# Ordering the second weight tile's conversion behind the first block's mean subtraction instead of behind the scaling of its input

## The chip, the cores and the metric

The kernel runs on one core of one Trainium2 chip. The metric is the device time of one execution in microseconds (us). Five engines matter: PE (TensorE, matrix products), DVE (VectorE), ACT (ScalarE), POOL (GpSimd) and SP, which here only issues transfers. Each engine works through its own instruction list in order.

## The reference

Three stages follow each other for 4 batches of 576 tokens.

```python
# 1. causal attention with a decay, 8 heads of 64
decay = cum[:, :, :, None] - cum[:, :, None, :]      # cum = cumsum(log f)
scores = np.where(causal, -1e9, q @ k.T / 8 + decay)
attn = softmax(scores);  x = concat_heads(attn @ v)  # 512 wide
# 2. normalised MLP, 512 -> 2048 -> 512
xn = (x - mu) / np.sqrt(var + 1e-6) * g_ln
x = x + np.maximum(xn @ w_ch1, 0.0) @ w_ch2
# 3. gated MLP with a product over the sequence
h = np.maximum(x @ w_in, 0.0);  u, v = split(h)
out = (u * (w_spatial @ layernorm(v) + b)) @ w_out
```

The weights arrive as float64 (two 32-bit words each) and are turned into float32 on the chip.

## The kernel before

**Blocks and groups.** The attention output is made in blocks of 256 tokens (`BLOCKS`), eight in all, and a ninth of the left-over tokens. The MLP of stage 2 runs on groups of blocks (`GROUPS`). Group 0 is block 0 alone and computes in float32; the later groups use pairs of float16 halves. Block 0 and block 1 hold the first 128 queries of two batches each (`attention32`, four head pairs); the next blocks use `attention1` and `attention`.

**Weight tiles.** The two weights of stage 2 are cut into 16 tiles (j = 0 to 15). Each tile is 1 MB of float64: `load_raw` loads it in two transfers into one of three buffers (`raw`), and `load_w` calls `narrow`, which has five steps:

- ACT takes the absolute value of the high words into `wt` (line 530, "Abs")
- ACT converts the low words into `low` (line 531)
- DVE clips `wt` (line 532)
- DVE puts the sign into `low` (line 533)
- DVE combines both into the float32 weight in `wt` (line 534)

In group 0 the hidden layer's products for tile j (line 707, into `ph`) and the second layer's (line 692, into `acc`) read the float32 weight. ACT's Relu (line 714) stands between them, and the second layer runs two tiles behind the first (`AHEAD`). After each conversion `squares(j)` multiplies the tile with itself (line 568, into `gram`); after tile 15 one small product of line 587 (`sums`) gives the scale of the weights, and `make16` (ACT line 597, DVE line 600) turns the tiles into float16 halves for group 1. On DVE, line 718 makes the low half of group 1's hidden layer.

**The norm of a block.** `norm` averages with a product (line 610), subtracts the mean with four DVE instructions (line 624), squares (ACT line 627), adds the squares on POOL (lines 631 and 632) and averages again (line 610). For group 0 `split` multiplies the centred block with the norm's gain g into `xg` (ACT line 671, four instructions); the products of line 707 read `xg`. The attention of a block ends with a copy of its last head pair into `xT` (ACT line 381).

**What sets the order.** `run` writes the steps down in the order of a list of due times (`SPAN`, `CONV`, `BEGIN`), and a scheduler with its own model of durations then sets the final order on each engine. `after(later, earlier)` adds an edge to it that keeps two instructions of one engine in order and makes no wait of its own. `PACE[j]` names the instruction behind which tile j's Abs must come: a place in `self.done`, or a name in `self.marks`. The mark "split" is the last scaling into `xg`.

Of the kernel before, what the change touches and what calls it, by code (L numbers as in the profile page):

```python
# [13 lines left out]
AF = mybir.ActivationFunctionType  # L14
ALU = mybir.AluOpType
# [38 lines left out]
SPAN.append((SPAN[-1][1] - 0.034, SPAN[-1][1] + 0.02))  # L54
RAWAT = (-0.975, -0.974, -0.973)
CONV = (-0.6, 0.001, 0.002, 0.003, 0.004)
PACE = (1, "split", "split", "split", "split")
LOWAT = (1, 2, 3)
SUMS = 13
SOON = 5  # L60
# [5 lines left out]
F64_LO = 2.0 ** -15  # L66
# [3 lines left out]
F64_HI = 2.0 ** 17 * (1 - 2.0 ** -5 - 2.0 ** -24)  # L70
# [10 lines left out]
def words(raw, w, dt):  # L81

    return raw.bitcast(dt).rearrange("p (n w) -> p n w", w=2)[:, :, w]


class Kernel:
# [236 lines left out]
    def attention32(self, b, xT):  # L323
        nc, at, bufs = self.nc, self.at, BUFS0
        mm = nc.tensor.matmul

        def bank(tag):
            return self.bank(tag).rearrange("p (b u w) -> p b u w", b=2, u=2)

        def four(tag):  # L330
            return at.tile([P, 2, 2, P], F32, tag=tag, name=tag, bufs=bufs[tag])
# [17 lines left out]
        for p in range(NP):  # L349
            qk, vr = qka[:, p], vra[:, :, p * P : (p + 1) * P]  # L350
            ps, e, diag = bank(tags[0]), four("e"), four("diag")
            st = at.tile([P, 2, 4], F32, tag="st", name="st", bufs=bufs["st"])
            four_ = [(n, u, 2 * n + u) for n in range(2) for u in range(2)]
            for n, u, c in four_:
                mm(ps[:, n, u], lhsT=qk[:, u, n, :P], rhs=qk[:, u, n, P:], start=True, stop=True, skip_group_check=True)
            for n, u, c in four_:
                mn, sm = st[:, 0, c : c + 1], st[:, 1, c : c + 1]
                nc.vector.tensor_tensor_reduce(
                    out=e[:, n, u], in0=ps[:, n, u], in1=self.mask[:, 512:], scale=-0.125, scalar=3e38, op0=ALU.add, op1=ALU.min, accum_out=mn)
                ex = nc.scalar.activation(e[:, n, u], e[:, n, u], AF.Exp, bias=mn, scale=-1.0, accum_out=sm)  # L360
                if b:
                    self.after(ex, self.marks["split"])
            nc.scalar.activation(st[:, 1], st[:, 1], AF.Copy, bias=1e-9)
            nc.vector.reciprocal(st[:, 1], st[:, 1])
            yield

            ps, pt = bank(tags[1]), four("PT")
            nc.vector.tensor_tensor(
                out=diag.rearrange("p n u w -> p (n u) w"), in0=self.ident.unsqueeze(1).broadcast_to([P, 4, P]),
                in1=st[:, 1].unsqueeze(2).broadcast_to([P, 4, P]), op=ALU.mult)  # L370
            for n, u, c in four_:
                mm(ps[:, n, u], lhsT=e[:, n, u], rhs=diag[:, n, u], start=True, stop=True, skip_group_check=True)
            copied = nc.scalar.activation(pt, ps, AF.Copy)
            if not b:
                self.done.append(copied)
            pav = bank("s2" if p % 2 and not b else tags[2])
            for n in range(2):

                for u in (1, 0):
                    mm(pav[: 64 * u + 64, 0, n], lhsT=vr[:, n, : 64 * u + 64], rhs=pt[:, n, u], start=True, stop=True, skip_group_check=True)  # L380
            nc.scalar.activation(xT[:, p].rearrange("p (n w) -> p n w", n=2), pav[:, 0], AF.Copy)
            if p == 1:
                xs = self.mo_sum(xT)
            elif p == 2:
                nc.vector.tensor_tensor(out=xs, in0=xs, in1=xT[:, 2, :], op=ALU.add)
            yield
# [130 lines left out]
    def narrow(self, raw, tmp, low=None):  # L517

        nc = self.nc
        a, b = tmp, tmp.bitcast(U32)  # L520
        lo, hi = words(raw, 0, U32), words(raw, 1, U32)
        if low is None:
            first = nc.scalar.activation(a, words(raw, 1, F32), AF.Abs)
            nc.vector.tensor_scalar(out=a, in0=a, scalar1=F64_LO, scalar2=F64_HI, op0=ALU.max, op1=ALU.min)
            nc.vector.tensor_scalar(out=b, in0=b, scalar1=3, scalar2=0x3FFFFFFF, op0=ALU.logical_shift_left, op1=ALU.bitwise_and)
            nc.vector.scalar_tensor_tensor(out=b, in0=hi, scalar=0xC0000000, in1=b, op0=ALU.bitwise_and, op1=ALU.bitwise_or)
            nc.vector.scalar_tensor_tensor(out=b, in0=lo, scalar=29, in1=b, op0=ALU.logical_shift_right, op1=ALU.bitwise_or)
        else:

            first = nc.scalar.activation(a, words(raw, 1, F32), AF.Abs, scale=2.0**16)  # L530
            self.low = nc.scalar.activation(low.bitcast(I32), lo, AF.Copy, scale=LOW)
            nc.vector.tensor_scalar(out=a, in0=a, scalar1=F64_LO * 2.0**16, scalar2=F64_HI * 2.0**16, op0=ALU.max, op1=ALU.min)
            nc.vector.scalar_tensor_tensor(out=low, in0=hi, scalar=0x80000000, in1=low, op0=ALU.bitwise_and, op1=ALU.bitwise_or)
            nc.vector.scalar_tensor_tensor(out=b, in0=b, scalar=3, in1=low, op0=ALU.logical_shift_left, op1=ALU.bitwise_or)
        return first
# [11 lines left out]
    def load_w(self, j):  # L547

        nc = self.nc
        if j not in self.raw:  # L550
            self.load_raw(j)
        raw, w = self.raw.pop(j), self.wt[:, j + 2]
        first = self.narrow(raw, w, self.st.tile([P, 2 * DM], U32, tag="low", name="low", bufs=2))
        at = PACE[j] if j < len(PACE) else NP + j - len(PACE)
        if at is not None:
            self.after(first, self.marks[at] if isinstance(at, str) else self.done[at])
        if j < len(LOWAT):
            self.after(self.low, self.done[LOWAT[j]])

# [53 lines left out]
    def norm(self, x, s, y, whole, end, c):  # L613


        nc, ns = self.nc, self.ns
        tag = "s" if end else "av"
        if s is None:
            pm = self.mean(tag, *(x[:, t] for t in range(NK)))
        else:  # L620
            nc.vector.tensor_tensor(out=s, in0=s, in1=x[:, 3, :], op=ALU.add)
            pm = self.mean(tag, s)
        for t in range(NK):
            nc.vector.tensor_tensor(out=c[:, t, :], in0=x[:, t, :], in1=pm, op=ALU.subtract)
        yield
        sq = ns.tile([P, NK, TOK], F32, tag="sq", name="sq", bufs=2)
        nc.scalar.activation(sq, c, AF.Square)
# [616 lines left out]
```

## Time and profile before

| What | Value |
|---|---|
| Median of 3 runs | 793.95 us (788.86 to 796.59) |
| The profiled execution | 790.01 us, of which the span is 788.3 us |
| PE busy | 761.2 us (97% of the span) |
| PE weight loads | 579.6 us (74%) |
| DVE busy | 555.3 us (70%) |
| ACT busy | 515.6 us (65%) |
| POOL busy | 59.7 us (8%) |

Shares are means over the whole span; the stages have different limits. The ends of PE's products are modelled, so a product's duration is longer than the spacing to the next. A float32 product leaves two records on PE, so "x8" of such products stands for four instructions of the program.

### The profile page before, as it was taken

How to read it: one execution, taken by the hardware profiler on the slowest of the kernel's cores; microseconds unless marked ns; L12 is line 12 of the kernel's file. 1: busy time of each engine (PE TensorE's matmuls, PEld its weight loads, DVE VectorE, ACT ScalarE, POOL GpSimd, SP SyncE). 2: the span in 40 equal slices, each digit the busy share in tenths (PEclk: the TensorE clock that was granted, in tenths of full speed). 3: DMA queues.
4: the chain of work that ended last, by engine and by line, in shares of the span. 5: the costliest groups of instructions: out<-in, count | busy, mean ns of one | idle time of the engine just before them, and what ended most of it. 6: DMA issues, size and time to landing. Idle time of an engine off the chain costs nothing.

```text
span 788.3 us, 16305 instructions
## 1 busy us (share of the span) xinstructions
PE 761.2 (97%) x5978; PEld 579.6 (74%) x5978; DVE 555.3 (70%) x1502; ACT 515.6 (65%) x1303; POOL 59.7 (8%) x89
## 2 busy tenths in 40 slices
PE   8799998999999999999999999999999999999997
PEld 6588887887877877778788888544447768667686
DVE  6699589849398989979958856687515672755725
ACT  5787389749388889888859844475425754556442
POOL 3100011011011001110201100100020000000000
PEclk8999999999999999999999999999999999999999
DMA  8888586367679997997995955730043230100101
GB/s 254 230 301 304 172 229 92 57 161 109 169 184 168 201 223 158 201 208 145 195 183 119 132 82 181 195 128 27 1 87 65 63 102 1 38 24 16 46 1 61
DMA packets 164227, 104.72 MB, mean 133 GB/s; under 512 B 106178, under 2 KB 151362, under 8 KB 164148
## 3 DMA queue, kind: packets, MB, share of 16 engines
q1 hardware_dynamic: 157848, 96.63, 50.8%
q0 software_dynamic: 5296, 5.28, 5.3%
q10 hardware_dynamic: 1004, 1.78, 0.8%
q8 instruction: 47, 0.77, 0.4%
q14 instruction: 32, 0.26, 0.1%
HBM read 64.37 MB, written 15.11 MB: 101 GB/s over the span
## 4 chain that ended last, share of the span: by engine, by line
PE 65%; DVE 12%; ACT 9%; DMA 8%; issue 3%; SPq 1%; POOL 1%; DVEq 0%; ACTq 0%; POOLq 0%
PE ph L707 15%; PE acc L692 13%; PE pb L647 8%; PE pb L648 8%; PE pb L649 8%; PE av L459 3%; PE s L295 2%; DMA PT<-P 2%; DVE P L316 2%; DMA vr<-in_v_dram 2%; PE s L692 1%; DVE sd L299 1%; ACT wt L597 1%; PE av L380 1%; DMA raw<-in_moe_w_in_dram 1%
## 5 line engine op out<-in xcount | busy, mean ns | idle before, releaser
L692 PE MATMUL acc<-hh,wt 128*128 128x256 f16 (+2 forms) x960 | 197.0, 295 | 0.8 <-DVE t L735 0.5
L707 PE MATMUL ph<-xh,wt 128*128 128x256 f16 (+1 forms) x896 | 186.7, 288 | 5.2 <-DVE hl L718 5.0
L707 PEld LDWEIGHTS <-wt 128*128 128x128 f16 x1344 | 126.8, 98 | 51.3 <-issue 13.2
L692 PEld LDWEIGHTS <-wt 128*128 128x128 f16 x1344 | 128.7, 98 | 43.9 <-issue 5.4
L707 PE MATMUL ph<-xl,wt 128*128 128x256 f16 (+1 forms) x448 | 129.0, 288 | 0.0
L692 PE MATMUL acc<-hl,wt 128*128 128x256 f16 (+1 forms) x416 | 115.2, 281 | 0.4 <-DVE hl L718 0.4
L714 ACT ACTIVATE hh<-ph 128x256 f16<-128x256 f32 (+2 forms) x128 | 51.0, 399 | 58.7 <-PE ph L707 58.5
L718 DVE SCALAR_TENSOR_TENSOR hl<-ph,hh 128x256 f16<-128x256 f32 (+1 forms) x112 | 50.6, 453 | 39.8 <-ACT hh L714 39.4
L260 ACT ACTIVATE P<-sd,st 128x512 f16<-128x512 f32 (+1 forms) x128 | 70.5, 586 | 10.5 <-DVE st L306 9.2
L316 DVE SCALAR_TENSOR_TENSOR P<-sd,st,P 128x384 f16<-128x384 f32 (+1 forms) x96 | 58.6, 633 | 9.3 <-ACT P L260 8.8
L303 ACT ACTIVATE sd<-sd,st 128x384 f32<-128x384 f32 (+2 forms) x80 | 54.5, 682 | 14.6 <-DVE st L299 14.3
L295 PE MATMUL s<-x 68*128 68x384 f32 (+7 forms) x256 | 63.2, 359 | 0.1
L299 DVE CUSTOM_DVE_ANT_0 sd<-s,mask 128x384 f32<-128x384 f32 (+2 forms) x80 | 45.8, 579 | 4.5 <-PE s L295 3.3
L739 POOL DMA_DIRECT2D x_d<-t x36 | 32.4, 1085 | 187.6 <-DVE t L735 149.8
L260 ACT ACTIVATE x<-qk 64x320 fp32r<-64x320 f32 (+1 forms) x64 | 41.3, 697 | 1.2 <-DMA qk<-in_qk_dram 1.2
L990 DVE SCALAR_TENSOR_TENSOR u<-pb,wsc,u 128x288 f32<-128x288 f32 x32 | 15.9, 514 | 32.9 <-PE pb L989 32.9
L295 PEld LDWEIGHTS s<-x 68*128 68x128 f32 (+3 forms) x256 | 36.9, 178 | 2.4 <-issue 0.6
L648 PE MATMUL pb<-x2l,wih 128*128 128x288 f16 (+2 forms) x144 | 37.8, 273 | 0.0
L647 PE MATMUL pb<-x2h,wil 128*128 128x288 f16 (+2 forms) x144 | 37.8, 273 | 0.0
L649 PE MATMUL pb<-x2h,wih 128*128 128x288 f16 (+2 forms) x144 | 37.8, 273 | 0.0
L647 PE MATMUL pb<-wsh,vl 128*128 128x288 f16 x128 | 36.6, 286 | 0.2 <-DVE x2s L204 0.2
L649 PE MATMUL pb<-wsh,vh 128*128 128x288 f16 x128 | 36.6, 286 | 0.0
(280 smaller groups left out, 1592.9 us busy)
## 6 DMA issues: line engine op xcount, KB each, us to landing
raw<-in_moe_w_ch_dram SPq DMA_DIRECT2D x32, 512.0 KB
qk<-in_qk_dram SPq DMA_DIRECT2D x32, 448.0 KB
vraw<-in_v_dram SPq DMA_DIRECT2D x5, 1024.0 KB
vr<-in_v_dram SPq DMA_DIRECT2D x16, 320.0 KB
x_d<-xT SPq DMA_DIRECT2D x9, 512.0 KB
x_d<-t POOLq DMA_DIRECT2D x36, 128.0 KB, 4.4
out_dram<-o SPq DMA_DIRECT2D x32, 144.0 KB
raw<-in_moe_w_in_dram SPq DMA_DIRECT2D x8, 512.0 KB
```

Of the source, the lines that this page charges most:

```text
L260: self.nc.scalar.activation(out, in_, AF.Copy, scale=scale)
L295: nc.tensor.matmul(ps[: R * u + R, : c1 - c0], lhsT=x[:, lo - q0 - R * u : hi - q0], rhs=y[:, c0:c1], start=g == 0, stop=g == len(heads[u] ...
L299: nc.vector.tensor_tensor_reduce(out=sd[:M, c0:c1], in0=ps[:M, : c1 - c0], in1=mask, scale=-0.125, scalar=3e38 if n == 0 else st[:M, n - 1 ...
L303: nc.scalar.activation(sd[:M, :N], sd[:M, :N], AF.Exp, bias=st[:M, n : n + 1], scale=-1.0, accum_out=st[:M, 2:3])
L316: low = nc.vector.scalar_tensor_tensor(out=dl, in0=src, scalar=rs, in1=dh, op0=ALU.mult, op1=ALU.subtract)
L647: first = mm(out, lhsT=al, rhs=bh, start=start, stop=False, **kw)
L648: mm(out, lhsT=ah, rhs=bl, start=False, stop=False, **kw)
L649: mm(out, lhsT=ah, rhs=bh, start=False, stop=stop, **kw)
L692: ins = nc.tensor.matmul(acc[m], lhsT=a, rhs=b, start=bank not in clear, stop=last and e == len(terms) - 1, skip_group_check=True)
L707: ins = nc.tensor.matmul(ph, lhsT=a, rhs=b, start=k == e == 0, stop=k == NK - 1 and e == len(terms) - 1)
L714: relu = nc.scalar.activation(hh, ph, AF.Relu)
L718: nc.vector.scalar_tensor_tensor(out=hl, in0=ph, scalar=0.0, in1=hh, op0=ALU.max, op1=ALU.subtract)
```

## The change

The mark "copied" is set to each attention copy of `attention32` as it is written down, the mark "centred" to each mean subtraction. When tile 1 is written down, they stand for block 0's last copy and its last subtraction. Tile 1's Abs is now kept behind the copy, on ACT, and its clip behind the subtraction, on DVE. Before, its Abs was kept behind the last scaling into `xg`. Tiles 2 to 4 stay behind "split".

```diff
-PACE = (1, "split", "split", "split", "split")
+PACE = (1, "copied", "split", "split", "split")
...
-            nc.scalar.activation(xT[:, p].rearrange("p (n w) -> p n w", n=2), pav[:, 0], AF.Copy)
+            self.marks["copied"] = nc.scalar.activation(xT[:, p].rearrange("p (n w) -> p n w", n=2), pav[:, 0], AF.Copy)
...
-            nc.vector.tensor_scalar(out=a, in0=a, scalar1=F64_LO * 2.0**16, scalar2=F64_HI * 2.0**16, op0=ALU.max, op1=ALU.min)
+            self.clip = nc.vector.tensor_scalar(out=a, in0=a, scalar1=F64_LO * 2.0**16, scalar2=F64_HI * 2.0**16, op0=ALU.max, op1=ALU.min)
...
+        if j == 1:
+            self.after(self.clip, self.marks["centred"])
...
-            nc.vector.tensor_tensor(out=c[:, t, :], in0=x[:, t, :], in1=pm, op=ALU.subtract)
+            self.marks["centred"] = nc.vector.tensor_tensor(out=c[:, t, :], in0=x[:, t, :], in1=pm, op=ALU.subtract)
```

The scheduler's order changes with it, from here up to the end of the attention. Lines behind 556 have a number higher by two in the changed kernel.

ACT from block 0's last attention copy on, before (`wt<-raw` is Abs, `low<-raw` the low words, `hh` the Relu of group 0, `y` the norm, `e,st` the softmax of block 1):

```order
L381 ACTIVATE xT<-s_349 128x256
L671 ACTIVATE xg<-xT,gT 128x256 x3
L627 ACTIVATE sq<-xT 128x1024
L671 ACTIVATE xg<-xT,gT 128x256
L530 ACTIVATE wt<-raw 128x1024 x3
L360 ACTIVATE e,st<-e,st 128x128 x4
L714 ACTIVATE hh<-ph 128x256
L635 ACTIVATE y<-av,eps 128x256
L531 ACTIVATE low<-raw 128x1024
L363 ACTIVATE st<-st 128x4
L530 ACTIVATE wt<-raw 128x1024
```

The same stretch of ACT in the changed kernel:

```order
L381 ACTIVATE xT<-s_349 128x256
L530 ACTIVATE wt<-raw 128x1024
L673 ACTIVATE xg<-xT,gT 128x256 x3
L629 ACTIVATE sq<-xT 128x1024
L673 ACTIVATE xg<-xT,gT 128x256
L530 ACTIVATE wt<-raw 128x1024 x2
L360 ACTIVATE e,st<-e,st 128x128 x4
L531 ACTIVATE low<-raw 128x1024
L716 ACTIVATE hh<-ph 128x256
L530 ACTIVATE wt<-raw 128x1024
L531 ACTIVATE low<-raw 128x1024
L363 ACTIVATE st<-st 128x4
```

Tile 1's Abs stands ahead of the four scalings and the square, the Abs of tiles 2 and 3 behind them, and tile 3's low words ahead of the first Relu.

DVE from block 0's mean subtraction on, before:

```order
L624 TENSOR_TENSOR xT<-xT,av 128x256 x4
L532 TENSOR_SCALAR wt<-wt 128x1024
L534 SCALAR_TENSOR_TENSOR wt<-wt,low 128x1024
L532 TENSOR_SCALAR wt<-wt 128x1024 x2
L534 SCALAR_TENSOR_TENSOR wt<-wt,low 128x1024
L533 SCALAR_TENSOR_TENSOR low<-raw,low 128x1024
```

The same stretch of DVE in the changed kernel:

```order
L626 TENSOR_TENSOR xT<-xT,av 128x256 x4
L532 TENSOR_SCALAR wt<-wt 128x1024
L534 SCALAR_TENSOR_TENSOR wt<-wt,low 128x1024
L532 TENSOR_SCALAR wt<-wt 128x1024
L534 SCALAR_TENSOR_TENSOR wt<-wt,low 128x1024
L532 TENSOR_SCALAR wt<-wt 128x1024
L533 SCALAR_TENSOR_TENSOR low<-raw,low 128x1024
```

The clip and combination of tile 1 keep their place; tile 3's clip moves behind tile 2's combination. On PE, tile 1's `squares` and its four products of line 707 stand ahead of the second mean of the norm (line 610) instead of behind it, and the four second-layer products of tile 0 behind the first-layer products of tile 2.

PE around the sums product of line 587, before (`acc` and `ph` are the second and first layer of group 0, `av<-PT,vr` the attention output of block 1):

```order
L692 MATMUL acc<-hh,wt 128x256 x2
L707 MATMUL ph<-xg,wt 128x256 x2
L380 MATMUL av<-PT,vr 128x128
L380 MATMUL av<-PT,vr 64x128
L380 MATMUL av<-PT,vr 128x128
L380 MATMUL av<-PT,vr 64x128
L707 MATMUL ph<-xg,wt 128x256 x2
L692 MATMUL acc<-hh,wt 128x256 x2
L587 MATMUL gram<-gss,ones 128x2
L692 MATMUL acc<-hh,wt 128x256 x2
L707 MATMUL ph<-xg,wt 128x256 x4
```

The same place of PE in the changed kernel:

```order
L694 MATMUL acc<-hh,wt 128x256 x10
L380 MATMUL av<-PT,vr 128x128
L380 MATMUL av<-PT,vr 64x128
L380 MATMUL av<-PT,vr 128x128
L380 MATMUL av<-PT,vr 64x128
L589 MATMUL gram<-gss,ones 128x2
L709 MATMUL ph<-xg,wt 128x256 x8
L694 MATMUL acc<-hh,wt 128x256 x2
```

Counted from the start, 52 products of line 707 and 42 of line 692 stand ahead of the sums product before, and 52 and 50 in the changed kernel.

DVE at group 1's first low half of the hidden layer (`hl`), before (`wt<-wt,w1c` and `w2c` are conversions of `make16`, `vs` and `vsc` scales of the values):

```order
L600 SCALAR_TENSOR_TENSOR wt<-wt,w1c 128x512
L204 TENSOR_SCALAR vsc<-vgram 128x4
L204 TENSOR_SCALAR vs<-s_1195 128x1
L600 SCALAR_TENSOR_TENSOR wt<-wt,w2c 128x512
L718 SCALAR_TENSOR_TENSOR hl<-ph,hh 128x256 x2
L206 TENSOR_SCALAR vs<-vs 128x1
```

The same place of DVE in the changed kernel:

```order
L415 RECIPROCAL st<-st 128x2
L204 TENSOR_SCALAR vsc<-vgram 128x4
L720 SCALAR_TENSOR_TENSOR hl<-ph,hh 128x256
L602 SCALAR_TENSOR_TENSOR wt<-wt,w1c 128x512
L720 SCALAR_TENSOR_TENSOR hl<-ph,hh 128x256
L205 TENSOR_SCALAR vs<-vs 128x1
```

Twenty of `make16`'s 32 conversions on DVE stand ahead of this first low half before, and 14 in the changed kernel.

## Rows read from the trace of the kernel before

**Rows 1.** Stretches: length, busy PE, PEld, DVE, ACT, POOL, then clock, DMA share, GB/s.

```profile
42.00:99.00 57.00, 57.00 (x375) 49.13 (x375) 45.24 (x79) 37.89 (x72) 0.00 (x0) 1.00 0.75 252
...
118.00:138.00 20.00, 17.53 (x162) 14.56 (x161) 20.00 (x57) 19.88 (x49) 3.59 (x4) 1.00 0.66 92
138.00:480.00 342.00, 333.33 (x3080) 274.72 (x3081) 268.61 (x752) 256.63 (x690) 32.02 (x46) 1.00 0.80 159
```

**Rows 2.** Chain that ended last, from 35 us: start, us, what.

```profile
35.05 1.03 ACT wt L530
...
36.11 1.27 DVE wt L532
...
37.41 1.24 DVE wt L534
...
38.69 1.04 PE gram L568 x8
39.72 2.98 PE ph L707 x8
42.70 1.73 PE acc L692 x8
44.42 0.46 PE gram L568 x8
44.88 1.78 PE ph L707 x8
```

**Rows 3.** Timeline, 30 to 37.5 us: start, us, instruction, idle before it.

```profile
30.01 0.38 ACT L381 ACTIVATE xT<-s 128x256 f32<-128x256 f32 x1 [0.71 <-PE s L380]
...
31.95 1.41 DVE L624 TENSOR_TENSOR xT<-xT,av 128x256 f32<-128x256 f32 x4
32.40 1.30 ACT L671 ACTIVATE xg<-xT,gT 128x256 f32<-128x256 f32 x3 [2.00 <-DVE xT L624]
...
34.74 1.27 POOL L631 TENSOR_TENSOR sq<-sq 128x512 f32<-128x512 f32 x1 [22.76 <-ACT sq L627]
34.96 3.19 ACT L530 ACTIVATE wt<-raw 128x1024 f32<-128x1024 f32 x3
...
35.10 0.70 PE L707 MATMUL ph<-xg,wt 128*128 128x256 f32 x2 [0.58 <-ACT xg L671]
36.09 0.73 POOL L632 TENSOR_TENSOR sq<-sq 128x256 f32<-128x256 f32 x1
36.10 0.37 SPq L542 DMA_DIRECT2D raw<-in_moe_w_ch_dram  x1
36.11 1.26 DVE L532 TENSOR_SCALAR wt<-wt 128x1024 f32<-128x1024 f32 x1 [2.75 <-ACT wt L530]
...
36.87 0.70 PE L610 MATMUL av<-sq,onesf 128*128 128x256 f32 x2 [1.07 <-POOL sq L632]
```

**Rows 4.** Single lines: duration in ns, min/median/max, over all instructions.

```profile
L532 DVE TENSOR_SCALAR wt<-wt x16: 661/685/1262, 22.2 to 89.5; 128x1024 f32<-128x1024 f32 x16
...
L531 ACT ACTIVATE low<-raw x16: 1114/1158/1185, 22.1 to 80.4; 128x1024 int32<-128x1024 uint32 x16
...
L360 ACT ACTIVATE e<-e,st x32: 384/386/418, 11.6 to 82.6; 128x128 f32<-128x128 f32 x32
...
L714 ACT ACTIVATE hh<-ph x128: 357/376/598, 39.6 to 574.5; 128x256 f16<-128x256 f32 x96, 128x256 f32<-128x256 f32 x16, 128x512 f16<-128x512 f32 x16
...
L600 DVE SCALAR_TENSOR_TENSOR wt<-wt,w1c x16: 735/741/1124, 100.6 to 142.4; 128x512 f16<-128x512 f32 x16
```

**Rows 5.** Single microseconds, columns as in the first group.

```profile
32.00:33.00 1.00, 0.04 (x1) 0.04 (x1) 1.00 (x6) 0.60 (x2) 0.00 (x0) 1.00 0.61 178
...
36.00:37.00 1.00, 0.13 (x1) 0.13 (x2) 0.89 (x1) 1.00 (x2) 0.74 (x2) 1.00 0.03 9
...
39.00:40.00 1.00, 1.00 (x8) 0.96 (x7) 1.00 (x3) 1.00 (x6) 0.00 (x0) 0.50 1.10 439
```

**Rows 6.** Timeline of PE at 99 us: the sums product.

```profile
99.20 0.28 PE L587 MATMUL gram<-gss,ones 128*128 128x2 f32 x2
```

## The prediction

> **What bounds the kernel now.** I read the table of stretches first, then the chain of waits, then the timeline where the change acts. PE is the engine to follow: from 42 to 99 us it is busy all the time, and from 138 to 480 us for 333.33 of 342 us [rows 1]. So time that PE loses early is lost for good unless a later stage waits for something else. One such stage shows: from 118 to 138 us DVE is busy for 20.00 and ACT for 19.88 of 20 us while PE idles for 2.47 [rows 1]. There the weights are turned into float16 halves for group 1, and that work starts with the sums product at 99.20 us [rows 6].
>
> At 35 us the chain leaves PE: Abs of tile 1 on ACT (35.05), its clip on DVE (36.11), its combination (37.41), and only then PE's product of the tile with itself (38.69) [rows 2]. Meanwhile PE has two gaps. Its last product of tile 0 ends at 35.10 + 0.70 = 35.80; the norm's second mean runs at 36.87 after 1.07 us idle and ends at 37.57; the tile's product follows 38.69 - 37.57 = 1.12 us later [rows 2, 3]. The gaps make 1.07 + 1.12 = 2.19 us. After them PE is slow for a while: at 39 us the granted clock is 0.50, which is 1.2 GHz, after a microsecond with PE busy for 0.13 [rows 5]. The tile's eight products with itself take 1.04 us where the next tile's take 0.46, and the first-layer products 2.98 where the next tile's take 1.78 [rows 2]. That is 0.58 + 1.20 = 1.78 us. Tile 1 thus costs PE 2.19 + 1.78 = 3.97 us.
>
> **The change, part by part.** *Abs of tile 1 on ACT.* It moves ahead of the four scalings. One Abs takes 3.19 / 3 = 1.06 us; the copy that it follows ends at 30.01 + 0.38 = 30.39, so it ends at 31.45. ACT waits there anyway, 2.00 us until the first subtraction lets the scaling start at 32.40 [rows 3]. Price nothing; the cover is that wait, and without it the 1.06 us would delay PE's first product. Tile 1 itself was loaded long before: its low words are converted ahead of that copy.
>
> *Clip behind the subtraction on DVE.* The subtractions end at 31.95 + 1.41 = 33.36, and DVE then idles for 2.75 us until the Abs is done [rows 3]. Now the clip runs at once: 0.69 us [rows 4], then the combination, 1.22 us, ends at 35.3, before PE is done with tile 0 at 35.80. Nothing is queued behind the new order that was not behind the old one.
>
> *PE.* Tile 1's products follow at 35.80 without a gap. With the full-speed prices of rows 2: its product with itself to 36.26, first layer to 38.04, the mean (POOL is done at 36.82) to 38.5.
>
> *Tile 2.* ACT reaches its Abs at 34.96 as first of two and ends it at 36.02; clip and combination end at 36.02 + 0.69 + 1.22 = 37.9. PE wants it at 38.5 and has it. Its products end at 38.5 + 0.46 + 1.78 = 40.75, tile 0's second layer at 42.5.
>
> *What is late next.* ACT's list sets it. After the two Abs (37.08) come four exponentials (4 x 0.386, to 38.62), tile 3's low words (1.16, to 39.78), tile 0's Relu (0.36, to 40.14), tile 4's Abs (1.06) and low words (1.16, to 42.36), a copy of 0.1 and tile 1's Relu, to 42.85 [rows 3, 4]. PE could start tile 1's second layer at 42.5, so 0.4 us of waiting is new. Tile 3's combination is done at about 43 on DVE and PE asks for it at 44.6. The gain is 3.97 - 0.4 = 3.6 us.
>
> *The loads.* Abs of tile 1 frees its buffer, so tile 4's two transfers leave SP's queue at about 31.5 instead of 36.10 [rows 3]. They stand behind the store of block 0, as before, and pass nothing. They then run beside the load of block 1's values, which PE needs only after block 1's first softmax. Price nothing.
>
> *POOL beside DVE.* Before, DVE was idle for most of the two POOL sums (34.74 to 36.82); now the combination of tile 1 and the clip of tile 2 run beside them. The trace has one such meeting: the clip at 36.11 met the second sum and took 1.26 us where the median is 0.685, 0.58 more [rows 3, 4]. The bounds are nothing and the whole of both sums, 1.27 + 0.73 = 2.00 us. I take 0.58, the only meeting of these lines: the combination then ends at 35.9, PE starts 0.1 later, and the 0.4 us at the Relu swallows it. With the whole 2.00 tile 2 is ready at 39.9 instead of 38.5, 1.4 late, of which 0.4 is swallowed: the gain falls to 2.6. The Trainium skill (SBUF — State Buffer, Who interferes with whom) speaks against this part of the change: whichever of a DVE instruction with two inputs in SBUF and a reading POOL instruction starts first holds the shared port for its whole length. By that rule the combination, which starts first, would hold POOL's first sum back to 35.3, and tile 2's clip would wait behind that sum; the sum of terms would lie between the two gains just given. The 0.58 us agrees with such a wait, but does not show who waits when DVE starts first.
>
> *From 42 to 99 us* PE had no gap, so its lead stays if the conversions keep up. They should: loads, Abs and combinations move ahead too.
>
> *The sums product.* It now stands behind eight more second-layer products. Four take 1.73 us [rows 2], so eight take 3.46. With PE 3.6 us ahead it runs at 99.20 - 3.6 + 3.46 = 99.1, the same moment as before. What hangs on it on ACT and DVE hence starts no earlier, though PE has 3.46 us less left of group 0. Whether the gain lives on depends on DVE's order: group 1's first low half stood behind 20 of the 32 conversions, now behind 14, six of 0.74 us or 4.4 us earlier [rows 4]. So PE gets group 1's work about as much sooner as it needs it, and I let it keep the 3.6 us.
>
> *Later.* The order differs up to about 470 us and is the same after it. I price that at nothing; bounds are below.
>
> **The sum.** 790.01 - 3.6 = 786.4 us for the profiled execution. That one lies 0.5% under the median of the runs, so I forecast 793.95 x 786.4 / 790.01 = **790.3 us**. Runs of this kernel differ by up to 1%, so that is about what a measurement can tell from no change.
>
> **The rivals.** *The gain is swallowed at 118 to 138 us.* If DVE and ACT, full there, set PE's end of that stretch and both start at 99.1, PE only idles longer: 2.47 + 3.5 us. For it: both are at 20 of 20 us [rows 1]. Against it: the six conversions. It gives 789.9, or 793.8 on the median.
>
> *The clock falls anyway.* At 32 us PE is busy for 0.04 of a microsecond and the clock holds; it falls after the gaps from 35.8 on [rows 5], and these are the ones that go. If it falls all the same, 1.78 us come back, less the 0.4 at the Relu that PE then meets late: gain 2.2, 787.8, or 791.7. The Trainium skill (TensorE: Matmul & The Clock Gate, Part 1: The HAM clock gate) says that the number of products at the low clock varies between runs of the same kernel; no run here shows it.
>
> *Slower: the sums product comes later than before.* Its place is PE's list at 99 us, its price the eight products ahead of it, 3.46 us, and it decides once PE's lead there is smaller than that and the full DVE sets the rest. With a lead of 2.2 us the sums run 1.3 us late, and so does everything behind: 791.3, or 795.2.
>
> *The new order up to 470 us is better or worse.* From 138 to 480 us PE idles for 342 - 333.33 = 8.67 us [rows 1]. If half goes, 782.1 (786.0); if it doubles, 795.1 (799.1). Nothing in the trace chooses.
>
> **How the numbers follow.** Forecast 0.50; swallowed 0.16; clock 0.12; sums late 0.08; later order 0.14, half to each side. The likeliest is 790.3. All but the last one's worse half lie between 786.0 and 795.2; the median of a few runs moves by some 2 us on top, so the range is 784 to 797. Every case priced lies within 1%. Faster by over 1% needs a better later order on top of the forecast, 0.07; slower by over 1% a worse one without the gain, 0.04; within 1% 0.89.
>
> **What would show it.** Abs of tile 1 ending before 32 us and its combination near 35.3 to 35.9; PE without a gap between tile 0's and tile 1's products, and at 2.4 GHz around 39 us; POOL's sums or DVE's clip lengthened near 35 to 37 us; the sums product at about 99 us; PE's idle time from 118 to 138 us near 2.5 us (forecast) or 6 us (swallowed). The forecast is wrong if PE waits for conversions between 50 and 99 us, or if the idle time behind 138 us changes by more than the 3.6 us won.

## The result and the profile after

The changed kernel takes 800.04 us (median of 20 runs, 796.72 to 801.89), the kernel before 794.2 us in 20 runs beside it: a ratio of 1.0072, with an interval of 1.0054 to 1.0090. The change makes the kernel 0.72%, or 5.7 us, slower, where a gain of 3.6 us was forecast. The profiled execution has a span of 798.4 us after 788.3.

At the place of the change the trace looks as forecast. Timeline of the changed kernel, 31 to 44 us (it answers [rows 3]; this execution was 1.26 us later already at ACT's copy in line 381):

```profile
31.27 0.38 ACT L381 ACTIVATE xT<-s 128x256 f32<-128x256 f32 x1 [0.70 <-PE s L380]
31.55 1.15 ACT L530 ACTIVATE wt<-raw 128x1024 f32<-128x1024 f32 x1
...
33.66 1.31 ACT L673 ACTIVATE xg<-xT,gT 128x256 f32<-128x256 f32 x3 [0.96 <-DVE xT L626]
...
35.26 1.22 DVE L534 SCALAR_TENSOR_TENSOR wt<-wt,low 128x1024 uint32<-128x1024 uint32 x1
...
36.00 1.62 POOL L633 TENSOR_TENSOR sq<-sq 128x512 f32<-128x512 f32 x1 [24.80 <-ACT sq L629]
...
36.37 0.70 PE L709 MATMUL ph<-xg,wt 128*128 128x256 f32 x2 [0.58 <-ACT xg L673]
...
36.91 0.62 PE L570 MATMUL gram<-wt 128*128 128x128 bf16 x8
...
37.37 1.94 PE L709 MATMUL ph<-xg,wt 128*128 128x256 f32 x8
...
37.39 0.78 DVE L532 TENSOR_SCALAR wt<-wt 128x1024 f32<-128x1024 f32 x1 [0.91 <-ACT wt L530]
37.70 1.06 POOL L634 TENSOR_TENSOR sq<-sq 128x256 f32<-128x256 f32 x1
38.21 1.64 DVE L534 SCALAR_TENSOR_TENSOR wt<-wt,low 128x1024 uint32<-128x1024 uint32 x1
...
41.30 1.99 PE L709 MATMUL ph<-xg,wt 128*128 128x256 f32 x8 [0.77 <-ACT hh L716]
```

Abs of tile 1 runs in ACT's wait, which shrinks from 2.00 to 0.96 us. The tile is combined 2.15 us earlier (35.26 after 37.41, [rows 2]) although everything started 1.26 us later. PE goes from tile 0's products to tile 1's without a gap, and the clock stays up (it answers [rows 5]):

```profile
36.00:37.00 1.00, 0.63 (x4) 0.49 (x5) 0.48 (x1) 1.00 (x2) 1.00 (x1) 1.00 1.00 344
39.00:40.00 1.00, 0.84 (x6) 0.41 (x5) 1.00 (x2) 1.00 (x7) 0.00 (x0) 1.00 0.99 332
```

The loss is made later. The stretches of the changed kernel (they answer [rows 1]):

```profile
42.00:99.00 57.00, 56.33 (x365) 48.86 (x364) 44.73 (x78) 37.45 (x73) 0.00 (x0) 1.00 0.74 245
118.00:138.00 20.00, 16.87 (x150) 13.89 (x148) 19.09 (x57) 17.91 (x51) 3.58 (x4) 1.00 0.55 109
138.00:480.00 342.00, 328.65 (x2992) 270.26 (x2992) 271.73 (x753) 259.21 (x693) 32.20 (x46) 0.99 0.78 156
```

From 118 to 138 us PE idles for 3.13 us (2.47 before), and DVE and ACT are no longer full. From 138 to 480 us it idles for 13.35 us (8.67 before), and the clock is no longer 1.00. Behind three waits of PE in that stretch it falls to 0.50. The three products that waited, and then two of the microseconds behind the first:

```profile
187.27 1.10 PE L406 MATMUL s<-qk 66*128 66x256 f32 x4 [2.69 <-DMA qk<-decay_d]
...
326.69 0.38 PE L694 MATMUL acc<-hh,wt 128*128 128x256 f16 x2 [1.56 <-ACT hh L716]
...
409.81 0.30 PE L459 MATMUL av<-PT,vp 128*64 128x320 f16 x1 [1.91 <-issue]
```

```profile
188.00:189.00 1.00, 1.00 (x9) 0.76 (x8) 1.00 (x4) 1.00 (x4) 0.00 (x0) 0.89 0.00 0
189.00:190.00 1.00, 1.00 (x6) 0.53 (x4) 1.00 (x5) 1.00 (x5) 0.00 (x0) 0.50 0.47 97
```

SP's queue shows why PE waits at 187 us: the load of the last decay (line 400) stands behind a transpose (line 423), in the old order ahead of it. The changed kernel, then the kernel before:

```profile
182.24 0.48 SPq L399 DMA_DIRECT2D qk<-in_qk_dram  x1
182.81 1.27 SPq L423 DMA_TRANSPOSE PT<-P  x1
184.13 0.43 SPq L400 DMA_DIRECT2D qk<-decay_d  x1
```

```profile
178.97 0.53 SPq L399 DMA_DIRECT2D qk<-in_qk_dram  x1
179.56 0.44 SPq L400 DMA_DIRECT2D qk<-decay_d  x1
...
180.56 20.45 SPq L423 DMA_TRANSPOSE PT<-P  x7
```

The sums product runs at 101.80 us (99.20 before, [rows 6]):

```profile
101.80 0.38 PE L589 MATMUL gram<-gss,ones 128*128 128x2 f32 x2
```

**PE's place at equal work.** One number tells most: when PE ends the same product in two traces. The table below gives that time minus the time of before, at points up to which PE has done the same products in both orders. An execution that is late at 34 us, ahead of all that differs, stays late, so the offset at 34 us (0.1 to 2.2 us) is taken off. For the changed kernel: 2.9 us ahead at 49 us, 2.0 at 124, 0.7 at 132 to 158, then behind by 2.7 at 213, 4.3 at 350 and 7.6 at 491 us, where the orders are the same again. The profiled execution of before took 790.01 us, where its 20 runs have a median of 794.2, and that of the changed kernel took 800.14, where the median is 800.04; so these numbers end larger than the 5.7 us of the runs. What counts is the step from one point to the next.

### The profile page after: what moved, and what is told of

It is laid out like the page before. It is cut to its first block, busy times and chain, and to the rows that moved or that the text cites. A ratio compares the mean times of both kernels' runs of the same rounds, so it can differ in the third digit from the quotient of the medians.

```text
span 798.4 us, 16307 instructions
## 1 busy us (share of the span) xinstructions
PE 767.0 (96%) x5978; PEld 583.9 (73%) x5978; DVE 557.1 (70%) x1502; ACT 515.5 (65%) x1303; POOL 60.2 (8%) x89
## 4 chain that ended last, share of the span: by engine, by line
PE 69%; DVE 9%; ACT 9%; DMA 7%; issue 3%; SPq 1%; POOL 1%; ACTq 0%; DVEq 0%; POOLq 0%
PE ph L709 16%; PE acc L694 15%; PE pb L649 8%; PE pb L650 8%; PE pb L651 8%; PE s L295 4%; PE av L459 3%; PE s L694 1%; DMA raw<-in_moe_w_in_dram 1%; DMA PT<-P 1%; DMA vr<-in_v_dram 1%; DVE wt L602 1%; DMA raw<-in_moe_w_ch_dram 1%; ACT P L260 1%; ACT x L260 1%
```

## The experiments

All these kernels fix the order by hand. The scheduler is run once with the old edges and once with the new ones; its two lists are joined, and every engine is tied to the joined list by edges that make no wait. In the traces the joined kernels follow the list that they were given: PE's records of e12_back165 are those of before, and those of e11_front165 are the changed kernel's, in the same order up to the seam at 165 us. In the edits, which are shortened here, `trace` builds the program with the new edges (`NEXT`) or the old ones (`LATE`), in the order of the lists that it is given.

```python
def join(first, then, cut):      # first's order up to the instruction cut, then's behind it
    n = [x[0] for x in first].index(cut) + 1
    have = {x[0] for x in first[:n]}
    return first[:n] + [x for x in then if x[0] not in have]
```

`old` and `new` are the lists, `I-465`, `I-1731`, `I-2206` PE products at 47, 141 and 165 us, `I-1049` the sums product. `move` puts one instruction ahead of another of its engine. Each kernel was timed in five rounds beside the kernel before, 6 to 12 runs of each.

| Run | Order | Ratio to before (interval) |
|---|---|---|
| e3_local | new to 47 us, then old | 0.9964 (0.9942 to 0.9986) |
| e1_front | new to 141 us, then old | 1.0027 (1.0007 to 1.0048) |
| e11_front165 | new to 165 us, then old | 1.0009 (0.9991 to 1.0027) |
| e2_back | old to 141 us, then new | 1.0081 (1.0053 to 1.0109) |
| e12_back165 | old to 165 us, then new | 1.0079 (1.0054 to 1.0105) |
| e8_middle | new from 141 to 258 us only | 1.0037 (1.0016 to 1.0058) |
| e4_three | new, three waits mended | 1.0059 (1.0028 to 1.0089) |
| e5_sums_back | e1, sums product earlier | 1.0043 (1.0028 to 1.0059) |
| e9_both_back | e1, sums and attention earlier | 1.0059 (1.0036 to 1.0081) |
| e7_sums_soon | e3, sums product earlier | 0.9973 (0.9953 to 0.9994) |
| e10_both_soon | e3, sums and attention earlier | 0.9988 (0.9967 to 1.0008) |
| e14_behind | e3, new from sums to 165 us | 1.0003 (0.9975 to 1.0031) |
| e15_ahead | new to the sums, then old | 1.0009 (0.9984 to 1.0033) |
| e13_dve_act | e11, DVE and ACT old from the sums | 1.0196 (1.0156 to 1.0236) |
| r1_redraw | old to 141 us, another draw behind | 1.0088 (1.0063 to 1.0112) |
| r4_redraw165 | the same draw, behind 165 us | 1.0086 (1.0058 to 1.0115) |
| r2_redraw | old to 141 us, a second draw | 1.0117 (1.0091 to 1.0142) |
| r3_redraw | old to 141 us, a third draw | 1.0102 (1.0080 to 1.0125) |

### In front of a point or behind it

```diff
+    nc = trace(shapes, NEXT, engines(join(new, old, "I-1731")))     # e1_front
+    nc = trace(shapes, NEXT, engines(join(old, new, "I-1731")))     # e2_back
+    nc = trace(shapes, NEXT, engines(join(new, old, "I-465")))      # e3_local
```

> Every engine follows the changed kernel's order up to the PE product at 141 us (just behind the stretch in which DVE and ACT are full), and the old order behind it; the same instructions are done at that point in both orders. Theory 1 (the loss is made behind 141 us, by waits of PE in the new order of the later groups): in the two traces PE reaches this point 0.5 us later than before, of which 1.27 was already there at 20 us, so 0.8 us are won up to here; 793.4 us, ratio 0.999. Theory 2 (the loss is made up to here, by the sums product behind eight more products and the full DVE): the whole loss of 5.8 us stays, about 800 us, ratio 1.007.

> The counterpart: the old order up to the PE product at 141 us, the changed kernel's order behind it; the change at 31 us is thus not in it. Theory 1: 8.8 - 0.5 = 8.3 us later than the old order from 141 to 480 us in the two traces, with 6.6 left by the medians (5.8 + 0.8): 800 to 802 us, ratio 1.008 to 1.010. Theory 2: nothing of the loss, 794 us, ratio 1.000.

> The changed kernel's order up to tile 3's last product with itself (47 us), the old order behind it: the change alone, without the reordering that follows from it. In the trace of the changed kernel PE is 1.64 us ahead there, or 2.9 without the 1.27 us by which it started late. Theory 1, with the lead kept: 794.2 - 2.9 = 791.3 us, ratio 0.996. If the lead is swallowed at 118 to 138 us, where DVE and ACT are full: 794, ratio 1.000. Theory 2 says nothing else than the first of these, since the sums product stands here behind 42 second-layer products as before.

e3_local says that the change does what it was to do: a ratio of 0.9964, or 2.9 us, which is as much as PE is ahead at 49 us (the interval goes from 1.1 to 4.6 us). e2_back has nothing of the change and loses 0.8%. So theory 1 holds for the greater part. But e1_front is not 0.1% faster, it is 0.3% slower, and its trace shows why one must look at the seam of such a join:

```profile
142.81 0.38 PE L217 MATMUL s<-vq,ones 128*128 128x1 f32 x2 [2.47 <-ACT vp L215]
```

At 141 us the new order has done six conversions fewer on ACT and four fewer on DVE than the old one. The join runs them ahead of what PE wants next. In the changed kernel this wait is 0.47 us. At 165 us the two orders differ by one ACT instruction, so the seam was moved there.

```diff
+    nc = trace(shapes, NEXT, engines(join(new, old, "I-2206")))     # e11_front165
+    nc = trace(shapes, NEXT, engines(join(old, new, "I-2206")))     # e12_back165
```

> As e1_front, with the seam between the two orders at a PE product at 165 us instead of 141 us. At 141 us the two orders have not done the same work on ACT: six conversions and two other instructions stand behind the point in the changed kernel and ahead of it in the old order; in the traces of e1_front, e5_sums_back and e9_both_back PE waits 2.47 us right there for ACT, with a slow clock behind it (4.4 us between 141 and 158 us). At 165 us one ACT instruction differs. If those 4.4 us are the seam's, the front of the new order costs what PE's lead says: 2.7 us ahead at 47 us, 0.9 us at 141 us, so 793.1 against 794 us, ratio 0.997 to 1.000. If they are the new order's own: 1.003 to 1.005 as e1_front, e5_sums_back and e9_both_back.

> The counterpart: the old order up to 165 us, the changed kernel's order behind it, none of the change itself. If the loss is the order behind 165 us: 5 to 8 us, ratio 1.006 to 1.010 (e2_back, with the seam at 141 us: 1.0081). If a part of e2_back's loss was its seam: 1.002 to 1.005.

e12_back165 loses as much as e2_back (1.0079 and 1.0081), and PE loses nothing right behind its seam. So the order behind 165 us costs 0.79%, 6.3 us. e11_front165 (1.0009) lies between its two cases, a little above the range of the first, and its interval overlaps that of e1_front, so the ratio alone does not prove the theory of the seam. Its trace shows a seam of its own: from 168 to 184 us PE loses 2.0 us, partly in waits for loads that PE has neither before nor in the changed kernel.

```profile
171.01 1.11 PE L406 MATMUL s<-qk 66*128 66x256 f32 x4 [0.35 <-DMA qk<-in_qk_dram]
...
173.55 1.13 PE L406 MATMUL s<-qk 66*128 66x256 f32 x4 [0.99 <-DMA qk<-in_qk_dram]
```

What the front costs is therefore better read ahead of that seam, at 158 us: of the 2.9 us 0.9 are left in e11_front165 and 0.7 in the changed kernel, so some 2 us are given back from 47 us on. With 0.7 us kept and 6.3 lost the change costs 5.6 us; 5.7 were measured. PE at equal work, in us later than before:

| Run | 49 | 124 | 132 | 158 | 213 | 350 | 491 us |
|---|---|---|---|---|---|---|---|
| after | -2.9 | -2.0 | -0.7 | -0.7 | +2.7 | +4.3 | +7.6 |
| e3_local | -2.9 | -2.9 | -2.9 | -3.1 | -3.5 | -0.7 | -0.6 |
| e11_front165 | -2.9 | -2.5 | -0.2 | -0.9 | +1.1 | +0.3 | 0.0 |
| e14_behind | -2.9 | -1.7 | +0.1 | 0.0 | +0.9 | +2.9 | +2.3 |
| e12_back165 | +1.4 | +1.4 | +1.4 | +1.3 | +3.4 | +8.7 | +11.9 |

The +1.4 us of e12_back165 at 49 us are a clock that stays low longer at tile 1 (0.50 still at 44 us, before up to 42) in the same order as before. Its profiled execution is the longest of its 12 runs (803.38 us, median 799.31). Its stretch from 138 to 480 us reads like that of the changed kernel, and its waits are PE's, for transposes, loads and ACT (the numbers are us in all, how many waits, the longest):

```profile
138.00:480.00 342.00, 327.37 (x2967) 268.83 (x2965) 268.23 (x750) 257.68 (x690) 32.88 (x46) 0.98 0.78 155
```

```profile
PE av L459 <- DMA PT<-P: 2.5, 2, 2.0
...
PE s L406 <- DMA qk<-decay_d: 1.7, 1, 1.7
PE acc L694 <- ACT hh L716: 1.6, 2, 0.8
```

### Is it these three waits?

```diff
+    move(order, "I-2225", "I-1805")     # SP: load of a decay, line 400, ahead of a transpose, line 423
+    move(order, "I-4534", "I-4248")     # ACT: Relu, line 716, ahead of attention weights, line 260
+    move(order, "I-4584", "I-4316")     # ACT: the same for the next Relu
+    move(order, "I-5671", "I-5672")     # PE: attention product, line 459, behind the products before its group
```

> The changed kernel's order throughout, with four instructions moved at the three places where PE waits and its clock falls to 1.2 GHz behind it: on SP one load of a decay ahead of a transpose (PE waits 2.69 us for it at 187 us), on ACT two Relus between the weights of the attention instead of behind them (PE waits 1.56 us at 326.7 us), on PE one attention product behind the eight second-layer and score products that follow it (1.91 us at 409.8 us). Theory 1 (these waits, with the slow clock behind each, are the loss): PE falls back by 4.0, 2.3 and 2.3 us over these places in the two traces, so up to 8.6 us come back: 791.4 to 794 us against 800.0, ratio to the kernel before 0.996 to 1.000. Theory 3 (the waits only show a loss whose cause lies elsewhere, a full ACT or DVE, and return at the next place): 798 to 800 us, ratio 1.005 to 1.007.

The waits went from where they were mended and came back near by; the ratio is 1.0059 after 1.0072, which the intervals don't tell apart. In the trace PE waits 2.09 us for a transpose up to 198.47 us and 1.87 us up to 413.19 us, and the clock falls four times between 138 and 480 us instead of three (this execution took 802.57 us, where the median is 797.59). Theory 3: no single wait is the loss. e8_middle says the same of the place:

```diff
+    order = join(old, join(new, old, "I-3692"), "I-1731")     # new only from 141 to 258 us
```

> The old order up to 141 us, the changed kernel's order from there to a PE product at 258 us, the old order behind that. In the trace of e2_back PE has fallen back by 4.5 of its 8.0 us at this point, with 1.5 us of that ahead of 141 us where the orders are the same. If the loss is made step by step over the whole stretch of 340 us: 796 to 797.5 us, ratio 1.003 to 1.005. If it is made mostly by the decay load and the transposes near 187 to 200 us: 799 us. If mostly behind 258 us: 793 to 794 us.

By the ratios about half of e2_back's loss is made in the first third of the stretch. The one trace of e8_middle shows it only in part: PE is 2.9 us late at 248 us, but 0.3 us at 480 us.

### Is it this order, or any other than the old?

```diff
-LOWAT = (1, 2, 3)
+LOWAT = (1, 2, 4)     # r1_redraw, r4_redraw165; (1, 2) in r2_redraw; PACE = (1, "split", "split", None, None) in r3_redraw
...
+    nc = trace(shapes, LATE, engines(join(old, other, "I-1731")))     # "I-2206" in r4_redraw165
```

> The old order up to 141 us, and behind it the order that the scheduler gives when a quite different edge is changed (the low words of tile 2 kept behind tile 3's products instead of behind tile 2's): as many instructions of PE stand in another place (2423) as with the change studied (2313). Nothing of the change itself is in it. If the change's own order is to blame (something that the earlier tile 1 brings with it): 793 to 794 us, ratio 1.000 with 0.002 either way. If the old order behind 141 us is simply one of the better ones that the scheduler can give, and any redraw loses: 796 to 801 us, ratio 1.004 to 1.010.

> A second redraw without the change: the old order up to 141 us, behind it the scheduler's order with the edge for the low words of tile 2 left out. r1_redraw took 1.0088 of the time before, and e2_back, with the order of the change studied, 1.0081. If the old order is one of the better ones that the scheduler can give: 796 to 801 us, ratio 1.004 to 1.010. If r1_redraw met a bad one by chance: 792 to 795 us, ratio 0.998 to 1.002.

> A third redraw without the change: the old order up to 141 us, behind it the scheduler's order with the edges for tiles 3 and 4 left out (1920 instructions of PE in another place). Same two cases: 796 to 801 us, or 792 to 795 us.

> r1_redraw with the seam at 165 us; in the trace of r1_redraw PE lost 4.2 us between 141 and 158 us, behind the seam. If the redraw itself loses behind that too (PE fell back by another 2.7 us to 480 us in that trace): 795 to 799 us, ratio 1.003 to 1.008. If r1_redraw's loss was the seam alone: 0.999 to 1.002.

Three draws that have nothing to do with the change cost 0.9 to 1.2%, the one of r1_redraw the same with its seam at 165 us. So it does not take the earlier tile 1 to spoil the later order: the old order is better than all four others that were tried. How much of it is the draw and how much the seam is not equally clear. r2_redraw and r3_redraw lose nothing in the first 25 us behind their seam. In the traces of r1_redraw and r4_redraw165 most of the loss lies right behind it: r1_redraw loses 3.6 us of its 7.6 by 155 us (a wait of 1.90 us for a transpose at 146.70), r4_redraw165 loses 4.4 of its 6.5 us by 184 us (a wait of 2.25 us for a load at 168.88, where r1_redraw has none). These two do not tell the price of their draw from that of a seam, and no draw but the changed kernel's was run without one. Each draw has its own waits; the worst of r3_redraw is a load again:

```profile
PE s L295 <- DMA x<-decay_d: 6.6, 2, 5.6
PE ph L709 <- DVE hl L720: 2.5, 3, 1.2
PE s L406 <- DMA qk<-decay_d: 2.3, 1, 2.3
```

### Where the gain goes between 47 and 165 us

```diff
+    move(order, "I-1049", "I-1227")      # e5_sums_back: on e1_front
+    move(order, "I-1049", "I-757")       # e7_sums_soon: on e3_local
+    for a in ("I-757", "I-758", "I-759", "I-760", "I-1049"):      # the attention products, line 380, and the sums product
+        move(order, a, "I-1164")         # e9_both_back: on e1_front
+    # e10_both_soon, on e3_local: the four ahead of "I-1088", the sums product ahead of "I-1156"
```

> As e1_front (the changed kernel's order up to 141 us, the old one behind it), but the sums product stands ahead of six of the second-layer products and four attention products that it was put behind, 4.0 us earlier by their durations; its input is ready by then (DVE ends it at 95.2 us in the trace of e1_front, the sums product runs at 99.96 us, and DVE idles for 5.1 us until it). e1_front lost 795.54 - 789.46 = 6.1 us against e3_local, from which it differs only between 47 and 141 us. Theory S (the late sums product makes this loss, since everything on ACT and DVE for group 1 hangs on it): most of it comes back, 790 to 792 us, ratio 0.996 to 0.998. Theory D (the order of DVE and ACT between the conversions makes it): 795 us, ratio 1.002 to 1.003, as before.

> As e3_local (the best so far, 789.46 us), with the sums product 2.7 to 3.3 us earlier still, ahead of four attention products, two first-layer and two second-layer products (by their durations 0.27 to 0.48 us each), right where its input is ready. Theory S: ACT and DVE start group 1's work that much earlier, and of PE's idle time from 118 to 138 us (2.2 us of gaps in e3_local) a part goes: 787.5 to 789 us, ratio 0.993 to 0.996. Theory D: no change, 789.5 us.

> As e1_front and e5_sums_back, but block 1's last four attention products move with the sums product, ahead of eight second-layer products, to the place that both have in the old order. In e5_sums_back the sums product ran 3.5 us earlier than in e1_front and changed nothing: ACT's first conversion stands behind ACT's copy of those four products, and ACT went on waiting for them (5.8 us after 5.5). Theory S2 (what holds ACT and DVE back is the later of the two, and both were put behind the second layer's products): ACT starts 3.5 us earlier; 791 to 793 us, ratio 0.998 to 1.000 after 1.0027 and 1.0043. Theory D (the order of DVE and ACT behind it makes the loss): 795 to 796 us, ratio 1.003 to 1.004.

> As e3_local, with block 1's last four attention products two first-layer and two second-layer products earlier and the sums product behind them, four first-layer and two attention-free second-layer products earlier than it stood: both where their inputs are ready. ACT and DVE can begin the conversions for group 1 some 2.5 us earlier than in e3_local. Theory S2: a part of PE's 2.2 us of waits from 118 to 138 us goes: 787.5 to 789 us, ratio 0.992 to 0.996 (e3_local 0.9964, e7_sums_soon 0.9973). Theory D: no change, 0.996 to 0.998.

Theory S fell at e5_sums_back: the sums product ran at 96.44 us instead of 99.88, and ACT still waited for the attention products ahead of it in its list. Waits of ACT from 95 to 142 us, e5_sums_back:

```profile
ACT xT L381 <- PE av L380: 5.8, 1, 5.8
```

Theory S2 fell at e9_both_back, where that wait is 2.08 us, and PE is 2.7 us ahead at 124 and 0.9 at 132 us as in e1_front. Nor did an earlier sums product help the better kernel (e7_sums_soon, e10_both_soon). e1_front, e5_sums_back and e9_both_back all carry the seam at 141 us, so their medians say little; what counts is that 1.8 to 1.9 us are lost between 124 and 132 us in all three, wherever the sums product ran. Three last runs:

```diff
+    kind = ("DVE", "Activation")         # e13_dve_act: order is e11_front165's
+    order = [x for x in order if x[1].name not in kind] + [x for x in join(new, old, "I-1049") if x[1].name in kind]
...
+    order = join(join(join(new, old, "I-465"), new, "I-1049"), old, "I-2206")     # e14_behind
...
+    order = join(new, old, "I-1049")                                              # e15_ahead
```

> As e11_front165, with the old order on DVE and ACT from the sums product to 165 us; PE, SP and POOL keep the changed kernel's order there. 103 instructions of DVE and 98 of ACT stand in another place, none of PE. e11_front165 took 1.0009 of the time before and e3_local 0.9964: 3.6 us are given back between 47 and 165 us. Theory D (the order of DVE and ACT behind the sums product gives it back): 0.995 to 0.998. Theory P (PE's own order, or what stands ahead of the sums product, does): 1.000 to 1.003.

> As e3_local up to the sums product (the change at 31 us, then the old order, the sums product at 96.5 us), with the changed kernel's order on all engines from there to 165 us and the old one behind that. Theory D, or PE's order behind the sums product: the gain is given back, 0.999 to 1.003. If the loss comes from what stands ahead of the sums product: 0.995 to 0.998.

> The changed kernel's order on all engines up to the sums product, which thus stands behind eight more second-layer products, and the old order behind it. Theory D, or PE's order behind the sums product: the gain is kept, 0.995 to 0.998. If the loss comes from what stands ahead of the sums product, as the prediction's slower rival had it: 0.999 to 1.003.

e14_behind comes nearest: old order and an early sums product up to it, new order from there to 165 us. The gain is not seen any more (1.0003, with an interval down to 0.9975), and PE loses 1.8 us between 124 and 132 us. It is not quite clean: 1.2 us of the lead go at 48 us, where its order is e3_local's (a wait of 0.96 us for line 368 that e3_local does not have), and 0.9 us behind its seam at 165 us. PE's waits from 95 to 165 us, e14_behind, then before:

```profile
PE ph L709 <- DVE hl L720: 2.4, 2, 1.3
PE av L431 <- DMA PT<-P: 1.1, 1, 1.1
PE s L217 <- ACT vp L215: 0.5, 1, 0.5
```

```profile
PE av L431 <- DMA PT<-P: 1.3, 1, 1.3
PE ph L707 <- DVE hl L718: 0.7, 1, 0.7
```

What grew is PE's wait for DVE's first low halves of group 1, line 720: 2.4 us after 0.7 (2.0 in the changed kernel). e15_ahead settles nothing: at its seam PE waits 3.02 us for ACT (line 215) and the clock falls. It does show what a late sums product costs when the rest of the order doesn't allow for it. e13_dve_act was a miss: with DVE and ACT in one order and PE in the other, PE waits at four kinds of places, 9.2 us in all from 95 to 165 us. The lists of the engines belong together and can't be judged one by one in this way.

## Why the prediction was wrong

**Right.** The Abs is hidden in ACT's wait, the tile is ready at 35.3 us on the timeline of before, PE's two gaps go and the clock holds. PE is 4.2 us ahead at tile 2's products (forecast 3.97), and PE waits for no conversion between 50 and 99 us. Of the 2.9 us of lead at 49 us 2.0 are left at 124 us; 0.67 us of it goes in a wait at 65.73 us for the softmax of a block (line 368).

**Mis-sized: the new wait at a Relu.** Forecast 0.4 us at tile 1's Relu. Measured: 1.3 us between there and 49 us, of which the row at 41.30 shows 0.77 at another place. Tile 2's first layer waits for a free buffer of `ph`, which tile 0's Relu gives back, and that Relu stands behind four exponentials and tile 3's low words. The gain was 2.9 us, not 3.6; the runs of e3_local alone can't tell the two apart (1.1 to 4.6 us).

**POOL beside DVE.** Forecast 0.58 us on DVE. Each time the two met, the one that started later got longer, by nearly as much as the other still had to run. POOL's first sum took 0.35 us more than in [rows 3] (tile 1's combination, which kept its 1.22 us, still ran for 0.48), tile 2's clip 0.10 more than its median (POOL's first sum, 0.23), POOL's second sum 0.33 more (that clip, 0.47), tile 2's combination 0.42 more (POOL's second sum, 0.55). The 0.58 us of before fit as well (0.71). The Trainium skill (SBUF — State Buffer, Who interferes with whom) has an exclusive lock, held for the whole instruction by whichever of the two starts first. These rows agree with it to 0.14 us, and they show what the prediction left open: when DVE starts first, POOL waits. On PE the trace shows 0.16 us of waiting for it, ahead of tile 2's product with itself at 39.90.

**The sums product.** Its price was right: 99.88 us in e1_front after 96.50 in e3_local is 3.4 us, 3.46 by the forecast. Its moment was not: 101.80 is 100.5 us on the timeline of before, 1.3 us later than before and not the same, as in the rival "the sums product comes later than before" with its lead of 2.2 us (PE's was 2.0 at 124 us). Its place didn't matter, though (e14_behind). What failed is the step behind it, "so PE gets group 1's work about as much sooner as it needs it". The six conversions were to bring group 1's first low half 4.4 us earlier. It came 0.6 us earlier: at 131.44, or 130.2 us on the timeline of before, after 130.83. In e14_behind it came 0.2 us later, although the sums product ran 1.8 us earlier. The changed kernel, then before:

```profile
131.44 0.42 DVE L720 SCALAR_TENSOR_TENSOR hl<-ph,hh 128x256 f16<-128x256 f32 x1
```

```profile
130.83 0.74 DVE L718 SCALAR_TENSOR_TENSOR hl<-ph,hh 128x256 f16<-128x256 f32 x2
```

PE loses 1.3 to 2.3 us between 124 and 132 us with the new order there (after, e11_front165, e14_behind), and most of the gain ends as in the rival "swallowed at 118 to 138 us", with DVE and ACT not full there. What holds the low half back in the new order stays open; e13_dve_act, which was to tell DVE and ACT from PE, does not.

**The step that failed: "The order differs up to about 470 us and is the same after it. I price that at nothing".** It costs 6.3 us (e12_back165). PE's idle time behind 138 us grew by 4.7 us (13.35 after 8.67), more than the 3.6 us that the prediction had named as a sign that it is wrong. The rival for it had the place right and the chance too low: 0.07 for a worse order, as if better and worse were even. All four other orders that were run are worse, by 0.8 to 1.2%. That the rival's 799.1 us is near the 800.04 measured is luck: it keeps the gain of 3.6 us, which does not last, and adds 8.67 us of idle time, where 4.7 came; and the range of 784 to 797 left it out. The rival also had the size by PE's idle time alone; the slow clock behind the waits had no term there. A fall such as the one at 188 us costs about 1.7 us by the windows of single microseconds (an estimate), and the profiled execution of the changed kernel has three in that stretch where that of before has none. Over all runs the difference is smaller: the mean granted clock is 0.986 in the 20 runs of the changed kernel and 0.988 in the 32 of before beside e1_front, which makes an estimate of some 2 us of 790.

## What to carry to other kernels

An edge given to a list scheduler changes all that it orders afterwards. Where the order in place is already a good one, the price of drawing it again (0.8 to 1.2% here in four draws of four, one of them with much of its loss at a seam) belongs in the sum ahead of a local gain, which was 0.4% here. To take the gain without the price, hold the order: the change with the old order behind it (e3_local) is faster than both kernels, 0.9964. When two orders are joined to find a loss, choose a seam at which every engine has done the same work, and look for a wait right there before the ratio is believed. Even then a seam can cost: at 165 us the lists differ by one instruction, and e11_front165 loses 2.0 us behind it.

## What the runs showed of the hardware

The clock did not answer equal waits equally. In the changed kernel and in e2_back PE waits 1.62 us for the same low half near 233 us, after the same products. The changed kernel, then e2_back, whose order there is the same:

```profile
234.29 0.27 PE L709 MATMUL ph<-xh,wt 128*128 128x256 f16 x1 [1.62 <-DVE hl L720]
```

```profile
233.92 0.32 PE L709 MATMUL ph<-xh,wt 128*128 128x256 f16 x1 [1.62 <-DVE hl L720]
```

The microsecond at 235 us has the clock at 2.4 GHz in the one and at 1.2 GHz in the other:

```profile
235.00:236.00 1.00, 1.00 (x11) 0.90 (x10) 1.00 (x3) 1.00 (x4) 0.00 (x0) 1.00 0.80 204
```

```profile
235.00:236.00 1.00, 1.00 (x7) 0.69 (x6) 1.00 (x2) 1.00 (x4) 0.00 (x0) 0.50 1.33 211
```

PE waits 1.62 us for this low half in five traces; behind it the clock falls in two (e2_back, e4_three) and holds in three (before, after, e12_back165). So a wait of PE has a price beyond its length that comes and goes. The Trainium skill (TensorE: Matmul & The Clock Gate, Part 1: The HAM clock gate) says that the number of products at the low clock varies between runs of the same kernel. The rows above are of different kernels, but the runs of one agree: the kernel before, beside e14_behind, has a mean granted clock of 0.993 in its shortest run (788.0 us) and of 0.981 in its longest (798.62 us). e3_local has one fall too, at 338 us, behind a wait of 2.56 us.
